# Gates as a diagonal factor in the turning of the dense rows, slot stores one by one, an early second weight group

## The chip, the cores and the metric

The kernel runs on one core of a Trainium2 chip. The metric is device microseconds for one execution, lower is better. The core has a matrix engine (PE, with its weight loads shown as PEld), a vector engine (DVE), an activation engine (ACT), a general engine (POOL), and a queue engine (SP) that issues most transfers. Each engine works through its own instructions in program order, and waits on semaphores of the others.

## The reference

Three stages stand one behind the other, all in float32:

```python
# 1: attention with heads mixed before and after the softmax (4 batches, 12 heads, 448 tokens, 64)
scores = scale * q @ k.T ; scores = einsum('bhij,hg->bgij', scores, w_pre)
attn = softmax(scores)   ; attn = einsum('bhij,hg->bgij', attn, w_post) ; x = attn @ v   # 1792 x 768
# 2: one of 8 experts for each row
logits = normalize(x) @ normalize(expert_emb).T / tau
e = argmax(logits) ; gate = softmax(logits)[e]
x = gate * (relu(x @ w1[e]) @ w2[e])          # w1: 768 x 1024, w2: 1024 x 768
# 3: a dense block
h = x @ w_in ; out = (h - tanh(h)) @ w_out    # w_in: 768 x 2048, w_out: 2048 x 768
```

## The kernel before

**Precision.** Most products run on pairs: a value is split into a rounded high part (ACT copy to fp32r) and a low part (a subtraction on DVE or POOL), and three matmuls (high·high, high·low, low·high) are added up in PSUM. Plain float32 products and turnings by the identity stand beside them.

**Attention** runs in 180 blocks of up to ten query rows of all heads. The scores go through SBUF to a relay transfer on SP, then to the product with w_pre (line 373), the exponential on ACT (line 380), the product with w_post (line 412) and the product with v. At the start, `load_k` brings the keys of four head pairs into four buffers and the last two follow in the loop over pairs; `prep_en` prepares the expert embeddings (its two loads on SP, a square and a root on ACT, a chain of small DVE operations).

**Experts.** Nine items follow: eight experts with room for 256 rows each, and one item for overflow rows ("o"). Rows are fetched by an indirect gather on POOL, turned, multiplied with w1 in eight chunks `h_chunk` (each ends in an ACT relu, line 729), then with w2 in `y_half`. The weights of the next item are loaded by SP (`feed1`, `feed2`) as buffers come free and split on ACT and DVE (`do1`, `do2`). In the chunk loop `pump()` advances a generator by two steps a chunk: it works out the gate and the slot of each row (`emit_G`, `emit_ov`), stores both to DRAM as `sg_d` (twenty small stores on SP, lines 636 and 638, five between two yields), and prepares the overflow item (`ov_src`). Leftover conversion work on w_in and w_out runs in `conv_step`.

**Overflow item.** The results of all experts lie in `y_d` at slots, not yet multiplied by their gates. While the overflow item runs, POOL gathers the rows of the first half of the tokens (seven tiles of 128, `y0_gathers`), in token order. `y0_piece(j, hf)` multiplies tile j in place by its gates (`y_scale`, on DVE for j under 4 and on POOL for the others, line 846), turns three blocks of it by the identity and splits them into the tiles that held w1. These pieces stand between the matmuls of the overflow item (`ov_mid`), with the splits of the first w_in group (`wi0_split`). Then comes a branch, `tc.If(again > 0)`, for a second and further overflow tile and a fuller first half; this input doesn't enter it.

**Dense block.** It has 16 groups (j): two halves of 896 tokens, eight groups of 256 hidden columns. A group has four steps x of `stageA` (18 matmuls each, then ACT: square, tanh, two more squares, then a chain of six DVE operations), and between them 14 calls of `stageB` for the group before (six matmuls each, added up by DVE, line 1391). `between(x, chain)` also carries the splits of the next w_in and w_out group (`work`, line 1322 on ACT and 1323 on POOL), and the pieces of the second half's rows: `y_start` gathers, `y_piece` scales (every second tile on POOL) and turns them, three tiles in group 2, two at the end of group 7 and two at the start of group 8. Dependencies are tracked by tile; the order on each engine is that of the program.

Of the kernel before, what the change touches and what calls it, by code (L numbers as in the profile page):

```python
# [8 lines left out]
F32 = mybir.dt.float32  # L9
# [21 lines left out]
def body(ctx: ExitStack, tc, q, k, v, w_pre, w_post, emb, tau, w1, w2, win, wout, out):  # L31
# [4 lines left out]
    DM = H * D  # L36
# [93 lines left out]
    if True:  # L130
# [5 lines left out]
        LAG = 2  # L136
        NSR = 8
        nat = {}

# [8 lines left out]
        def load_k(b, p):  # L148
            t = ap.tile([CP, NJ, 2, D], F32, tag="natk", name=f"natk{b}_{p}", bufs=4)
            for hh in range(2):  # L150
                sp.dma_start(t[:, :, hh, :], k[b, 2 * p + hh].rearrange("(p c) d -> p c d", c=NJ))
            nat["k", b, p] = t
# [10 lines left out]
        load_q(0, 1)  # L163
        for p in range(1, 4):
            load_k(0, p)
        make_identity(nc, ident)

# [44 lines left out]
        ids0 = cp.tile([128, 1], I32, name="ids0")  # L212
        taub = cp.tile([128, 1], F32, name="taub")
        rtau = cp.tile([128, 1], F32, name="rtau")
# [40 lines left out]
        def prep_en():  # L255
            e0, e1 = xbuf[1][:E], xbuf[0][:E]
            sp.dma_start(e0, emb)
            sp.dma_start(taub, tau.to_broadcast([128, 1]))
            yield
            dve.reciprocal(rtau, taub)  # L260
            yield
            ess = cp.tile([E, 1], F32, name="ess")
            act.activation(e1, e0, AF.Square, accum_out=ess)
            yield
            for rn in inv_norm(ess, E, 1, "e"):
                yield
            dve.tensor_scalar(e1, e0, rn, rtau[:E], ALU.mult, ALU.mult)
# [309 lines left out]
        def emit_ov():  # L577
# [54 lines left out]
            for b in range(B):  # L632
                for it, (i0, n) in enumerate(IT):
                    nb = n // 10
                    r0, t = b * S + i0, 4 * b + it
                    sp.dma_start(sg_d[r0:r0 + 10 * nb, :].rearrange("(m r) k -> r m k", r=nb), sgp[:10 * nb, t, :])
                    if n % 10:
                        sp.dma_start(sg_d[r0 + 10 * nb:r0 + n, :], sgp[10 * nb:n, t, :])
                yield

    with mctx:
        mp, mq = [None], [None]
        keep = {}

        def ld1(src, nm, lo=0, hi=KD):
# [35 lines left out]

        def xsplit(xhl, t, j, hf, nm):
            pt = ps("e" if hf else "d", f"xt{nm}_{j}_{hf}")
            for c in range(3):
                cc = 3 * hf + c
                pe.transpose(pt[:, c * 128:(c + 1) * 128], t[:, cc * 128:(cc + 1) * 128], ident)
# [155 lines left out]

        def y_scale(t, j, eng):
            eng.tensor_scalar(t, t, sgn[:, j, 1:2], None, ALU.mult)  # L846

        def y0_piece(j, hf):
            if hf == 0:
                y_scale(yg0[j], j, dve if j < 4 else pool)  # L850
            xsplit(keep["w1"], yg0[j], j, hf, "y0")

        def wi0_split(x):
            sl = (slice(None), slice(3 * x, 3 * x + 3))
            act.copy(keep["wi0"][0][sl], raw6[sl])
            pool.tensor_sub(keep["wi0"][1][sl], raw6[sl], keep["wi0"][0][sl].bitcast(F32))

        def y0_again():
            yg0.clear()
            y0_gathers()  # L860
            for j in range(HJ):
                for hf in range(2):
                    y0_piece(j, hf)
            for x in range(2):
                wi0_split(x)

# [16 lines left out]

        osrc = []

        def tables():
# [196 lines left out]
        for p in range(NP):  # L1083
            if p + 4 < NP:
                load_k(0, p + 4)
            if p == 1:
# [106 lines left out]
        for n, e in enumerate(items):  # L1193
# [11 lines left out]
            elif e == OV:  # L1205
                y0_gathers()
                d2 = lambda f: lambda: do2(n, f, w2c)
                for f in range(4):
                    do2(n, f, w2c)
                t0 = h_over(hhl, w1c, xhl, 0, nm, {3: [d2(4)]})  # L1210
                t1 = h_over(hhl, w1c, xhl, 1, nm, {1: [d2(5)], 2: [t0], 4: [d2(6)]})
                do2(n, 7, w2c)
                keep["wi0"] = xtile("wi0")
                y0 = [lambda j=j, hf=hf: y0_piece(j, hf) for j in range(HJ) for hf in range(2)]
                ov_mid = [{2: [t1], 3: y0[0:1], 4: y0[1:2], 5: y0[2:3] + [lambda: wi0_split(0)], 6: y0[3:4], 7: y0[4:5]},
                          {f: y0[5 + f:6 + f + f // 7] + ([lambda: wi0_split(1)] if f == 2 else []) for f in range(KF)}]
            else:
                for f in range(KF):
# [4 lines left out]
                    if n == 6:  # L1223
                        pump(100)
                    if n == 7 and f == 2:
                        sp.dma_start(sgn, sg_d.rearrange("(j q) k -> q j k", q=128))
                    if f % 3 == 1:
# [27 lines left out]
        while ncv[0] < NCV or cst:  # L1255
            conv_step()
        again = nc.values_load(ovi[0:1, 2:3], min_val=0, max_val=1)
        with tc.If(again > 0):
            nov = nc.values_load(ovi[0:1, 0:1], min_val=0, max_val=NOV)
            with tc.For_i(1, nov, 1) as ko:  # L1260
                over_alone(ko, "ov")
            y0_again()


    with ExitStack() as dctx:
# [16 lines left out]
        def y_start(j):  # L1282
            yg1[j] = dp.tile([128, DM], F32, tag="yg", name=f"yg{j}", bufs=3)
            y_gather(yg1[j], j)

        def y_piece(j, hf):
# [111 lines left out]
        orr = wo_load(0, act)  # L1398
        wr = wi_load(1, act)
        NG = NF // GF  # L1400
# [6 lines left out]
        for j, (hf, g) in enumerate(seq):  # L1407
# [4 lines left out]
            groups = [(t, nh) for t in range(HT // 128) for nh in range(2)] if prev is not None else []  # L1412
            work = []
            wo_n = wo_tile(g)
            for f in range(GF):
                work.append(lambda f=f, r=orr, w=wo_n: wsplit(w, r, slice(f, f + 1)))
# [55 lines left out]
```

## Time and profile before

| | |
|---|---|
| median of 3 runs | 1386.45 us (1385.5 to 1386.89) |
| the profiled execution | 1384.36 us |
| its span, first to last instruction | 1382.6 us |
| mean granted clock of PE | 0.979 |
| busy: PE, DVE, ACT, POOL | 95%, 72%, 53%, 37% |

The span is what the trace covers; what lies around it is 1.8 us. The profile shows each instruction's start and length on its engine, the line that made it, and for idle time what ended it. "PEclk" and the last columns of a window give the granted clock as a share of 2.4 GHz.

### The profile page before, as it was taken

Reading aid. Unit: us, or ns where it says so; the run is one execution under the profiler, and the core shown is the slowest. Engines: PE = TensorE matmul, PEld = TensorE weight load, DVE = VectorE, ACT = ScalarE, POOL = GpSimd, SP = SyncE. Lnnn points to the kernel's source line nnn. Section 1 sums busy time; section 2 is a strip of 40 time slices with the busy share of each in tenths; the row PEclk is TensorE's granted clock in tenths of the full one; section 3 lists DMA queues with packets and bytes.
Section 4 is the critical chain, followed back from the end, with each engine's and each line's share of the span. In section 5 each row is a group of like instructions: output and inputs, shape, how many; then the busy total and the mean of one; then the engine's idle time right before and its main releaser. Section 6 shows DMA issues by size and latency. Waiting matters only on the chain. (4 is left out here: it accounts for less than half of the span.)

```text
span 1382.6 us, 24798 instructions
## 1 busy us (share of the span) xinstructions
PE 1307.3 (95%) x9036; PEld 1137.6 (82%) x9036; DVE 1001.4 (72%) x2173; ACT 739.1 (53%) x1507; POOL 510.0 (37%) x515
## 2 busy tenths in 40 slices
PE   8999999999999999999799996977999959999998
PEld 5777776776777778999799995777999859999998
DVE  4776787678777767777477773855888737888886
ACT  5666666676666665544344452643444434544442
POOL 0233333333333345332122223633555432454442
PEclk9999999999999999999899999999999979999999
DMA  5886675567556577887787752411212213212102
GB/s 146 253 253 188 186 215 157 173 200 203 157 172 205 161 227 243 265 267 233 218 258 256 243 183 82 126 46 46 61 67 69 65 39 103 69 46 69 46 24 80
DMA packets 153060, 210.93 MB, mean 153 GB/s; under 512 B 57670, under 2 KB 113142, under 8 KB 152934
## 3 DMA queue, kind: packets, MB, share of 16 engines
q1 hardware_dynamic: 148912, 194.22, 45.7%
q0 software_dynamic: 2480, 12.19, 2.6%
q10 hardware_dynamic: 1542, 2.89, 0.6%
q8 instruction: 73, 1.20, 0.4%
q14 instruction: 53, 0.43, 0.1%
HBM read 135.71 MB, written 35.01 MB: 123 GB/s over the span
## 5 line engine op out<-in xcount | busy, mean ns | idle before, releaser
L412 PEld LDWEIGHTS T<-w,p 120*112 120x112 f32 (+1 forms) x1440 | 165.8, 177 | 63.9 <-issue 41.6
L122 POOL TENSOR_TENSOR cm<-cm,ct 128x256 f32<-128x256 f32 x96 | 71.3, 742 | 376.7 <-DVE ct L119 347.1
L412 PE MATMUL T<-w,p 120*112 120x120 f32 (+1 forms) x1440 | 185.1, 272 | 3.1 <-ACT A L417 1.5
L1333 POOL TENSOR_TENSOR gl<-th,gh 128x512 fp32r<-128x512 f32 (+1 forms) x64 | 78.1, 1221 | 268.7 <-ACT gh L1332 207.3
L380 ACT ACTIVATE p<-P,mx 120x448 f32<-120x448 f32 x180 | 114.2, 634 | 117.4 <-DVE mx L387 103.9
L373 PE MATMUL P<-sr,wpre 120*120 120x448 f32 x360 | 166.2, 544 | 1.4 <-ACT p L380 1.4
L1385 PE MATMUL o<-woh,gh 128*128 128x384 f32 x448 | 154.6, 345 | 0.0
L1354 ACT ACTIVATE u<-h 128x512 f32<-128x512 f32 (+1 forms) x64 | 35.0, 546 | 222.6 <-PE h L1352 222.6
L1386 PE MATMUL o<-wol,gh 128*128 128x384 f32 x448 | 152.7, 341 | 0.0
L1387 PE MATMUL o<-woh,gl 128*128 128x384 f32 x448 | 152.5, 340 | 0.0
L1391 DVE TENSOR_TENSOR acc<-acc,o 128x384 f32<-128x384 f32 x196 | 106.3, 547 | 60.3 <-PE o L1387 60.3
L377 DVE TENSOR_REDUCE mx<-P 120x1 f32<-120x448 f32 x180 | 111.4, 619 | 48.7 <-PE P L373 47.0
L417 ACT COPY A<-T 112x480 f32<-112x480 f32 x180 | 101.7, 565 | 15.4 <-PE T L412 14.9
L120 POOL TENSOR_TENSOR cm<-craw 128x256 f32<-128x256 f32 x96 | 64.7, 674 | 92.9 <-DMA craw<-in_moe_w_in 51.6
L726 PE MATMUL hi<-xhi,w1h 128*128 128x256 f32 x336 | 95.4, 284 | 0.0
L727 PE MATMUL hi<-xli,w1h 128*128 128x256 f32 x336 | 95.3, 284 | 0.0
L702 PE MATMUL ypi<-w2hi,hhi 128*128 128x384 f32 x272 | 95.3, 350 | 0.0
L728 PE MATMUL hi<-xhi,w1l 128*128 128x256 f32 x336 | 95.3, 284 | 0.0
L430 PEld LDWEIGHTS AV<-A,v 112*64 112x64 f32 x1536 | 73.9, 137 | 23.9 <-issue 11.4
L703 PE MATMUL ypi<-w2li,hhi 128*128 128x384 f32 x272 | 92.4, 340 | 0.2 <-DVE w2li L673 0.2
L704 PE MATMUL ypi<-w2hi,hli 128*128 128x384 f32 x272 | 92.3, 340 | 0.0
L121 POOL TENSOR_SCALAR cm<-cm 128x256 f32<-128x256 f32 x96 | 85.6, 891 | 8.4
(277 smaller groups left out, 3471.9 us busy)
## 6 DMA issues: line engine op xcount, KB each, us to landing
sr<-ssb SPq DMA_DIRECT2D x176, 210.0 KB
r<-in_moe_w SPq DMA_DIRECT2D x72, 384.0 KB
r<-in_moe_w SPq DMA_DIRECT2D x52, 512.0 KB
craw<-in_moe_w_in SPq DMA_DIRECT2D x48, 256.0 KB
craw<-in_moe_w_out SPq DMA_DIRECT2D x48, 256.0 KB
raw<-wi_d SPq DMA_DIRECT2D x15, 768.0 KB
wor<-wo_d SPq DMA_DIRECT2D x15, 768.0 KB
wi_d<-cm SPq DMA_DIRECT2D x48, 128.0 KB
```

The lines of the kernel that those rows point to most:

```text
L373: pe.matmul(pt[:n, :S], wpre[:n, :n], t[:n, :], start=True, stop=True)
L377: dve.tensor_reduce(mx[:n, 0:1], pt[:n, :S], op=ALU.max, axis=AX.X, negate=True)
L380: return lambda: act.activation(p[:n, :], pt[:n, :S], AF.Exp, bias=mx[:n, 0:1], scale=1.0, accum_out=mx[:n, 1:2])
L412: pe.matmul(pt[:CP, c * n:(c + 1) * n] if m == 10 else pv[:, c], p[:n, c * CP:(c + 1) * CP], w[:n, :] if m == 10 else wv, start=True, stop ...
L417: act.copy(A[T][:, :, :, 10 * r:10 * r + m], tev.pop(i)[1])
L702: pe.matmul(pt[:, :384], a, wh[:, n0:n0 + 384], start=f == 0, stop=False)
L726: pe.matmul(pt[:, :256], wh[:, sl], xh[:, c, :], start=c == 0, stop=False)
L727: pe.matmul(pt[:, :256], wh[:, sl], xl[:, c, :], start=False, stop=False)
L1385: pe.matmul(pt[:, :384], gh[:, sl], wo[0][:, f, n0:n0 + 384], start=f == 0, stop=False)
L1386: pe.matmul(pt[:, :384], gh[:, sl], wo[1][:, f, n0:n0 + 384], start=False, stop=False)
L1387: pe.matmul(pt[:, :384], gl[:, sl], wo[0][:, f, n0:n0 + 384], start=False, stop=f == GF - 1)
L1391: dve.tensor_add(ac[:, n0:n0 + 384], ac[:, n0:n0 + 384], pt[:, :384])
```

## The change

- **Gates.** A gate no longer multiplies the rows: `y_diag` writes the identity times the gates (128 x 128, on DVE), and the turning becomes a float32 product with that diagonal, so it turns and scales at once. For the first half all seven diagonals are made in the overflow item (`y0_diags`); in the dense block one diagonal is made one step ahead of its piece (`y_dg`).
- **Overflow item.** The last four w2 splits, the turnings of the hidden rows and the pieces stand in another order; the last two pieces come behind the overflow item's matmuls (`ov_end`).
- **Second w_in group.** It is loaded on SP ahead of the branch instead of on ACT behind it. A fall into the branch loads and splits the first group anew. In the first dense group the w_in splits come ahead of the w_out splits.
- **Slot stores.** The twenty stores of `sg_d` go into a list, and each chunk of the following items issues one (`sg_store`).
- **Start.** All six key pairs are loaded at once into six buffers; the embeddings and tau are loaded on ACT's queue; ACT does the embeddings' square and root first, and calls one exponential there.

```diff
         def load_k(b, p):
-            t = ap.tile([CP, NJ, 2, D], F32, tag="natk", name=f"natk{b}_{p}", bufs=4)
+            t = ap.tile([CP, NJ, 2, D], F32, tag="natk", name=f"natk{b}_{p}", bufs=NP)
...
-        for p in range(1, 4):
+        for p in range(1, NP):
             load_k(0, p)
+        act.dma_start(xbuf[1][:E], emb)
+        act.dma_start(taub, tau.to_broadcast([128, 1]))
...
         def prep_en():
-            sp.dma_start(e0, emb)
-            sp.dma_start(taub, tau.to_broadcast([128, 1]))
-            yield
-            dve.reciprocal(rtau, taub)
-            yield
             ess = cp.tile([E, 1], F32, name="ess")
             act.activation(e1, e0, AF.Square, accum_out=ess)
-            yield
-            for rn in inv_norm(ess, E, 1, "e"):
+            norm = inv_norm(ess, E, 1, "e")
+            next(norm)
+            act.activation(mxk[:, 0:1], carry[:, 0:1], AF.Exp)
+            yield
+            dve.reciprocal(rtau, taub)
+            yield
+            for rn in norm:
                 yield
...
-                    sp.dma_start(sg_d[r0:r0 + 10 * nb, :].rearrange(...), sgp[:10 * nb, t, :])
+                    sgst.append((sg_d[r0:r0 + 10 * nb, :].rearrange(...), sgp[:10 * nb, t, :]))
...
-                yield
...
-        def xsplit(xhl, t, j, hf, nm):
+        def xsplit(xhl, t, j, hf, nm, dg=None):
...
+                    pe.matmul(pt[:, c * 128:(c + 1) * 128], t[:, cc * 128:(cc + 1) * 128], dg, start=True, stop=True)
...
-        def y_scale(t, j, eng):
-            eng.tensor_scalar(t, t, sgn[:, j, 1:2], None, ALU.mult)
+        def y_diag(t, j):
+            dve.tensor_scalar(t, ident, sgn[:, j, 1:2], None, ALU.mult)
+            return t
...
-            if hf == 0:
-                y_scale(yg0[j], j, dve if j < 4 else pool)
-            xsplit(keep["w1"], yg0[j], j, hf, "y0")
+            xsplit(keep["w1"], yg0[j], j, hf, "y0", dg0[j])
...
+        def sg_store():
+            if sgst:
+                sp.dma_start(*sgst.pop(0))
...
-                t0 = h_over(hhl, w1c, xhl, 0, nm, {3: [d2(4)]})
-                t1 = h_over(hhl, w1c, xhl, 1, nm, {1: [d2(5)], 2: [t0], 4: [d2(6)]})
-                do2(n, 7, w2c)
+                t0 = h_over(hhl, w1c, xhl, 0, nm)
+                t1 = h_over(hhl, w1c, xhl, 1, nm, {2: [t0], 3: [y0_diags, d2(4)], 5: [d2(5)]})
...
-                ov_mid = [{2: [t1], 3: y0[0:1], 4: y0[1:2], 5: y0[2:3] + [lambda: wi0_split(0)], 6: y0[3:4], 7: y0[4:5]},
-                          {f: y0[5 + f:6 + f + f // 7] + ([lambda: wi0_split(1)] if f == 2 else []) for f in range(KF)}]
+                ov_mid = [{0: [d2(6)], 1: [d2(7)], 2: [t1], 4: y0[0:1], 5: y0[1:2] + [lambda: wi0_split(0)], 6: y0[2:3], 7: y0[3:4]},
+                          {f: y0[4 + f:5 + f] + ([lambda: wi0_split(1)] if f == 2 else []) for f in range(KF)}]
+                ov_end = y0[4 + KF:]
...
+        for fn in ov_end:
+            fn()
+        sp.dma_start(raw6, wi_d[:, 256:512].rearrange("(c p) f -> p c f", p=128))
         again = nc.values_load(ovi[0:1, 2:3], min_val=0, max_val=1)
...
-            if not hf:
-                y_scale(yg1[j], j, dve if l % 2 else pool)
...
-                pe.transpose(pt[:, c * 128:(c + 1) * 128], yg1[j][:, cc * 128:(cc + 1) * 128], ident)
+                pe.matmul(pt[:, c * 128:(c + 1) * 128], yg1[j][:, cc * 128:(cc + 1) * 128], dg1[j], start=True, stop=True)
...
-        wr = wi_load(1, act)
+        wr = raw6
...
+            if j:
+                work.extend(wos)
             if nx is not None:
...
+            if not j:
+                work.extend(wos)
...
+                nj = spread.get((j, x + 1) if x < 3 else (j + 1, 0))
+                if nj:
+                    y_dg(nj[0][0])
```

## Rows read from the trace of the kernel before

**Rows 1.** The page, 40 slices of the span, PE's granted clock in tenths.
```profile
PEclk9999999999999999999899999999999979999999
```
**Rows 2.** Waits of PE: waiter, releaser, us in total, times, longest.
```profile
PE yt L1293 <- POOL yg L846: 28.2, 4, 7.8
PE xti L688 <- DVE yi L715: 9.8, 1, 9.8
...
PE yt L1293 <- DVE yg L846: 4.3, 3, 1.9
...
PE h L1352 <- POOL wi1l L1323: 2.8, 2, 1.6
```
**Rows 3.** Timeline of ACT: the first relu of three items in a row.
```profile
633.33 0.38 ACT L729 ACTIVATE hhi<-hi 128x256 fp32r<-128x256 f32 x1 [1.63 <-PE hi L728]
...
681.31 0.38 ACT L729 ACTIVATE hhi<-hi 128x256 fp32r<-128x256 f32 x1 [2.17 <-PE hi L728]
...
716.59 0.38 ACT L729 ACTIVATE hhi<-hi 128x256 fp32r<-128x256 f32 x1 [1.63 <-PE hi L728]
```
**Rows 4.** Timeline of SP: the first slot stores.
```profile
644.48 3.08 SPq L636 DMA_DIRECT2D sg_d<-sgp  x4
```
**Rows 5.** Timeline of ACT: the cast of the next item's last w1 chunk.
```profile
671.01 1.04 ACT L669 CAST w1h<-r 128x1024 fp32r<-128x1024 f32 x1 [11.79 <-DMA r<-in_moe_w]
```
**Rows 6.** Transfers from 640 to 672 us, packets by size.
```profile
DMA packets 4333, 5.93 MB, mean 185 GB/s; under 512 B 2273, under 2 KB 2657, under 8 KB 4331
```
**Rows 7.** Timeline of ACT: the first square of dense groups 2, 3, 4, 7, 8, 9.
```profile
913.52 0.60 ACT L1354 ACTIVATE u<-h 128x512 f32<-128x512 f32 x1 [2.89 <-PE h L1352]
...
964.84 0.60 ACT L1354 ACTIVATE u<-h 128x512 f32<-128x512 f32 x1 [5.86 <-PE h L1352]
...
993.94 0.60 ACT L1354 ACTIVATE u<-h 128x512 f32<-128x512 f32 x1 [5.86 <-PE h L1352]
...
1081.22 0.60 ACT L1354 ACTIVATE u<-h 128x512 f32<-128x512 f32 x1 [5.85 <-PE h L1352]
...
1121.97 0.49 ACT L1354 ACTIVATE u<-h 128x384 f32<-128x384 f32 x1 [4.72 <-PE h L1352]
...
1164.04 0.49 ACT L1354 ACTIVATE u<-h 128x384 f32<-128x384 f32 x1 [4.34 <-PE h L1352]
```
**Rows 8.** Timeline of PE in group 2: the first piece.
```profile
921.43 0.90 PE L1293 MATMUL yt<-ident,yg 128*128 128x128 f32 x3 [6.89 <-POOL yg L846]
```
**Rows 9.** Timeline of POOL in group 2.
```profile
919.17 2.21 POOL L846 TENSOR_SCALAR yg<-yg,sgn 128x768 f32<-128x768 f32 x1
```
**Rows 10.** Timeline of PE in the attention stage: float32 products and turnings.
```profile
152.73 0.86 PE L464 MATMUL X<-ien,xT 128*120 128x136 f32 x6
153.43 0.92 PE L373 MATMUL P<-sr,wpre 120*120 120x448 f32 x2
...
162.87 0.47 PE L303 MATMUL ptq<-ident,natq 120*128 120x120 f32 x3
163.18 0.92 PE L373 MATMUL P<-sr,wpre 120*120 120x448 f32 x2
```
**Rows 11.** Window over the w2 matmuls of expert 7: us, busy (x) by engine, clock, DMA.
```profile
806.00:816.00 10.00, 10.00 (x60) 10.00 (x59) 6.29 (x8) 4.27 (x5) 0.73 (x1) 1.00 0.46 146
```
**Rows 12.** Timeline of DVE in the overflow item.
```profile
828.76 0.68 DVE L756 TENSOR_TENSOR hli<-hqi,hhi 128x512 fp32r<-128x512 f32 x1
829.61 0.96 DVE L673 TENSOR_TENSOR w2li<-r,w2hi 128x768 fp32r<-128x768 f32 x1 [0.16 <-ACT w2hi L669]
```
**Rows 13.** Groups by line: DVE's scaled 120 x 120 tiles of the attention.
```profile
L390 DVE TENSOR_SCALAR w<-wpost,mx 120x120 f32<-120x120 f32 x180 | 67.1, 373 | 6.3
```
**Rows 14.** Timeline of PE: the first dense matmul.
```profile
860.56 0.47 PE L1350 MATMUL h<-w1h,xhwi 128*128 128x512 f32 x1 [1.47 <-DVEq L1258]
```
**Rows 15.** Timeline of ACT at the first block's exponential.
```profile
25.48 1.28 ACT L380 ACT_TABLE_LOAD   x1
```
**Rows 16.** Window over dense group 4, columns as in rows 11.
```profile
993.94:1023.03 29.09, 29.09 (x158) 27.60 (x157) 24.76 (x38) 13.70 (x25) 16.96 (x12) 1.00 0.31 96
```

More of the change, by code (lines that the diff above doesn't have):

```diff
@@ L137, in body @@
         NSR = 8
+        taub = cp.tile([128, 1], F32, name="taub")
         nat = {}
@@ L212, in body @@
         ids0 = cp.tile([128, 1], I32, name="ids0")
-        taub = cp.tile([128, 1], F32, name="taub")
         rtau = cp.tile([128, 1], F32, name="rtau")
@@ L256, in prep_en @@
             e0, e1 = xbuf[1][:E], xbuf[0][:E]
-            sp.dma_start(e0, emb)
-            sp.dma_start(taub, tau.to_broadcast([128, 1]))
+            ess = cp.tile([E, 1], F32, name="ess")
+            act.activation(e1, e0, AF.Square, accum_out=ess)
+            norm = inv_norm(ess, E, 1, "e")
+            next(norm)
+            act.activation(mxk[:, 0:1], carry[:, 0:1], AF.Exp)
             yield
@@ L261, in prep_en @@
             yield
-            ess = cp.tile([E, 1], F32, name="ess")
-            act.activation(e1, e0, AF.Square, accum_out=ess)
-            yield
-            for rn in inv_norm(ess, E, 1, "e"):
+            for rn in norm:
                 yield
@@ L635, in emit_ov @@
                     r0, t = b * S + i0, 4 * b + it
-                    sp.dma_start(sg_d[r0:r0 + 10 * nb, :].rearrange("(m r) k -> r m k", r=nb), sgp[:10 * nb, t, :])
+                    sgst.append((sg_d[r0:r0 + 10 * nb, :].rearrange("(m r) k -> r m k", r=nb), sgp[:10 * nb, t, :]))
                     if n % 10:
-                        sp.dma_start(sg_d[r0 + 10 * nb:r0 + n, :], sgp[10 * nb:n, t, :])
-                yield
+                        sgst.append((sg_d[r0 + 10 * nb:r0 + n, :], sgp[10 * nb:n, t, :]))
     with mctx:
@@ L645, in body @@
         keep = {}
+        sgst = []
         def ld1(src, nm, lo=0, hi=KD):
@@ L687, in xsplit @@
                 cc = 3 * hf + c
-                pe.transpose(pt[:, c * 128:(c + 1) * 128], t[:, cc * 128:(cc + 1) * 128], ident)
+                if dg is None:
+                    pe.transpose(pt[:, c * 128:(c + 1) * 128], t[:, cc * 128:(cc + 1) * 128], ident)
+                else:
+                    pe.matmul(pt[:, c * 128:(c + 1) * 128], t[:, cc * 128:(cc + 1) * 128], dg, start=True, stop=True)
             pv = pt[:, :384].rearrange("p (c t) -> p c t", c=3)
@@ L843, in y_gather, with y0_diags, wi0_split @@
                                     in_offset=bass.IndirectOffsetOnAxis(ap=sgn[:, j, 0:1].bitcast(I32), axis=0))
-        def y_scale(t, j, eng):
-            eng.tensor_scalar(t, t, sgn[:, j, 1:2], None, ALU.mult)
+        def y_diag(t, j):
+            dve.tensor_scalar(t, ident, sgn[:, j, 1:2], None, ALU.mult)
+            return t
+        dg0 = []
+        def y0_diags():
+            t = mp[0].tile([128, DM], F32, tag="xg", name="dg0", bufs=3)
+            u = mp[0].tile([128, OT], F32, tag="osl", name="dg1")
+            for j in range(HJ):
+                dg0.append(y_diag(u if j == 6 else t[:, j * 128:(j + 1) * 128], j))
         def y0_piece(j, hf):
-            if hf == 0:
-                y_scale(yg0[j], j, dve if j < 4 else pool)
-            xsplit(keep["w1"], yg0[j], j, hf, "y0")
-        def wi0_split(x):
+            xsplit(keep["w1"], yg0[j], j, hf, "y0", dg0[j])
+        def wi0_split(x, r=None):
             sl = (slice(None), slice(3 * x, 3 * x + 3))
-            act.copy(keep["wi0"][0][sl], raw6[sl])
-            pool.tensor_sub(keep["wi0"][1][sl], raw6[sl], keep["wi0"][0][sl].bitcast(F32))
+            rv = raw6[sl] if r is None else r
+            act.copy(keep["wi0"][0][sl], rv)
+            pool.tensor_sub(keep["wi0"][1][sl], rv, keep["wi0"][0][sl].bitcast(F32))
         def y0_again():
             yg0.clear()
+            dg0.clear()
+            y0_diags()
             y0_gathers()
@@ L863, in y0_again @@
                     y0_piece(j, hf)
-            for x in range(2):
-                wi0_split(x)
         items = list(range(E)) + ["o"]
@@ L1083, in body @@
         for p in range(NP):
-            if p + 4 < NP:
-                load_k(0, p + 4)
             if p == 1:
@@ L1224, in body @@
                         pump(100)
+                    sg_store()
                     if n == 7 and f == 2:
+                        assert not sgst
                         sp.dma_start(sgn, sg_d.rearrange("(j q) k -> q j k", q=128))
@@ L1261, in body @@
                 over_alone(ko, "ov")
+            raw0 = mp[0].tile([128, FF], F32, tag="r1", name="raw0", bufs=NB1)
+            wiv = wi_d[:, :256].rearrange("(c p) f -> p c f", p=128)
+            for x in range(2):
+                rv = raw0[:, :DM].rearrange("p (c f) -> p c f", c=3)
+                sp.dma_start(rv, wiv[:, 3 * x:3 * x + 3, :])
+                wi0_split(x, rv)
             y0_again()
@@ L1284, in y_start, with y_dg @@
             y_gather(yg1[j], j)
+        dg1 = {}
+        def y_dg(j):
+            dg1[j] = y_diag(dp.tile([128, 128], F32, tag="dg", name=f"dg{j}", bufs=2), j)
         def y_piece(j, hf):
             l = j - HJ
-            if not hf:
-                y_scale(yg1[j], j, dve if l % 2 else pool)
             pt = psb(f"yt{j}_{hf}")
@@ L1412, in body @@
             groups = [(t, nh) for t in range(HT // 128) for nh in range(2)] if prev is not None else []
-            work = []
+            work, wos = [], []
             wo_n = wo_tile(g)
             for f in range(GF):
-                work.append(lambda f=f, r=orr, w=wo_n: wsplit(w, r, slice(f, f + 1)))
+                wos.append(lambda f=f, r=orr, w=wo_n: wsplit(w, r, slice(f, f + 1)))
+            if j:
+                work.extend(wos)
             if nx is not None:
```

## The prediction

> **What bounds the kernel now.** I read the page first. PE is busy for 95% of the span, so a gain can only come from places where PE stands still or runs at its lower clock. The clock line [rows 1] stays at 9 tenths or more except in slice 19 (from 656.7 us; a slice is 34.6 us) and slice 32 (from 1106 us): at the end of the experts' third quarter and at the change of the dense halves. The list of PE's waits [rows 2] says what ended its longest stands: 28.2 us in four waits on rows that POOL scales, 9.8 us in one wait in the expert stage, 4.3 us on rows that DVE scales, 2.8 us on low parts of w_in. The reader is to see that all of these belong to a few places, and that each has a lower clock behind it, so that a wait alone understates its price. I therefore price each place by a period: the distance of one marker to the next, less that of an undisturbed neighbour.
>
> **The slot stores.** From the first relu of one item to that of the next it is 35.28 us undisturbed (681.31 to 716.59) and 47.98 us (633.33 to 681.31) in the item that issues the twenty stores [rows 3]. The difference is 12.70 us. Four stores take SP 3.08 us, 0.77 us each [rows 4]; twenty in a row hold the queue for about 15 us, and the weight loads stand behind them in program order. ACT waited 11.79 us for the last w1 chunk of the next item [rows 5], and PE's 9.8 us [rows 2] end with the copy that frees PE's bank behind it. One store a chunk leaves at most eight in an item, 6.2 us of SP in 35.28 us, each behind one load and not ahead of six. I take the whole 12.7 us as gained; if the stores cost as much wherever they stand, it is 0. Four yields fewer let the overflow item's preparation run two chunks earlier; the pump is idle long before the item needs it, so this costs nothing.
>
> **The dense block's rows.** An undisturbed group takes 29.10 us (964.84 to 993.94) [rows 7]. Group 2, with three tiles, took 51.32 us: 22.2 us more. From the first square of group 7 to that of group 8 it took 40.75 us; group 8 begins with a chain of 384 columns where the others have 512, which is 18 matmuls x 128 columns at 2.4 GHz, 0.96 us, so 28.1 us would be undisturbed, and 12.6 us were lost. Group 8 to 9: 42.07 us, 13.0 us lost. Together 47.8 us [rows 7]. The first piece shows how: PE stood 6.89 us until POOL had scaled its tile [rows 8], and POOL began that 2.21 us operation only at 919.17 [rows 9], since it stands in POOL's queue behind the splits of the same step. The scaling leaves POOL altogether. What takes its place is a 128 x 128 scaling on DVE, nearest to the attention's 120 x 120 tiles at 0.37 us [rows 13], ordered one step (some 7 us) ahead of its piece. DVE is busy 24.76 us of 29.09 in a group [rows 16], so seven of these lie in its free time; without that cover they would cost 2.6 us.
>
> The turnings become dearer. Six records of a float32 product of 136 columns (two records for each product) take PE 0.70 us start to start (152.73 to 153.43); three turnings of 120 columns take 0.31 us [rows 10]. A piece of three products of 128 columns is then 0.70 x 128/136 = 0.66 us, and 14 pieces are 9.2 us that stay on PE. I add 1 us for banks that ACT and DVE free late. The dense rows gain 47.8 - 9.2 - 1 = 37.6 us; bounds are 38.6 us with no wait left, and 25 us if each of the seven tiles keeps 1.8 us (DVE's three waits of today are 1.4 us each [rows 2]).
>
> A rule of the Trainium skill speaks against this edit. On the page "TensorE: Matmul & The Clock Gate", section Terms, the transpose mode is four times as fast for float32 as the ordinary path. By it a piece would take 4 x 0.31 x 128/120, an estimate of 1.3 us, and the 28 pieces would lose some 18 us more than by the row. The attention's products show about twice a turning, not four times; it stays as a rival below.
>
> **The overflow item.** The first dense matmul starts at 860.56 [rows 14]. The new order puts seven diagonals (2.6 us), four w2 low parts (0.96 us each, 3.8 us) and the second low part of the hidden rows (0.68 us) in DVE's queue behind the first one, which ended at 829.44 [rows 12]. If none of it is hidden, PE gets its hidden rows at 836.5; if the diagonals lie in gaps, at 833.9. I take the middle, 835.2, because the relu ahead no longer stands behind a weight cast on ACT. From there PE has the last matmul of one w2 row (0.17 us; 60 matmuls take 10 us [rows 11]), eleven more rows of three matmuls (0.50 us), and thirteen pieces at 0.66 us: 0.17 + 5.5 + 8.6 = 14.3 us, until 849.5. The last piece's copy and low part and the branch follow; the branch alone cost 1.47 us [rows 14], so I take 2.0 us, and the dense block begins at 851.5. Gain 9.1 us, bounds 7.8 and 10.4. The rows were all gathered and are no longer scaled ahead of their turning; POOL keeps only the w_in splits.
>
> **First dense group.** The w_in splits come first and their load is on its way before the branch, so the 2.8 us of waits for w_in low parts [rows 2] go. But the w_out low parts now stand last in POOL's queue, behind the same activations, and the second group's first sums need them. The stall moves from one product to the next. I take 0; bounds are a gain of 4 us and a loss of 2 us. SP's extra load ahead of the branch lies beside the last pieces, and what SP has behind it waits for nothing else.
>
> **Start.** A table load of 1.28 us stands ahead of the first exponential [rows 15]; the early exponential moves it into the start, where ACT has nothing before the first keys have been turned. Part of it lay beside DVE's first maximum. I take 0.6 us, between 0 and 1.3. If the embeddings land late, ACT's early square holds up the first key copies; that costs at most about 1 us, and the six key pairs and two more buffers change nothing that PE waits for.
>
> **The sum.** 12.7 + 37.6 + 9.1 + 0 + 0.6 = 60.0 us. The profiled execution took 1384.36 us, so 1324.4 us; the median of the runs shown is 2.1 us above that execution, so I predict 1326.5 us.
>
> **Rivals.**
> - *A new wait takes the place of POOL's.* In a step with a piece, DVE's queue holds the low part of the piece, which waits for ACT's copy, which stands behind four activations and the weight casts. If PE then waits 1.8 us for each dense tile, 12.6 us are given back: 1339 us. For it: the tiles that DVE scaled had waits too [rows 2]. Against it: those waited for the scaling itself.
> - *The small stores are dear as transfers.* Of the packets around them 2273 of 4333 are under 512 B [rows 6]. If it is these packets and not SP's issuing that held up the weights, spreading gains nothing: 1339 us. Against it: SP issued stores for the whole stretch [rows 4]. The Trainium skill ("DMA: Bandwidth & Descriptors", Specifications) says that under 512 B an engine reads, modifies and writes; this trace has no price for one such packet.
> - *A product costs four times a turning:* 18 us of the gain are lost, 1344 us. Against it: [rows 10]. It decides nothing on the sign.
> - *Slower.* The diagonals stand in DVE's queue behind sums that wait for PE. If each of the 14 tiles made PE wait for its diagonal, the sum turns at 60.0/14 = 4.3 us a tile, and the kernel is measurably slower from 4.5 us. At a whole step of 7.3 us for each it would be 102 us lost and 1428 us. Against it: DVE has 4.3 us free in each group [rows 16], and in the overflow item all seven diagonals come ahead of the first piece.
> - *The gates stay in the way.* If the first pieces waited for the gathers themselves, the scaling would gain nothing but its own time. Against it: POOL's scaling could start at 919.17 only with its rows landed, while the four POOL waits end with POOL.
>
> **How the numbers follow.** The forecast has 0.62, the new wait 0.17, the dear stores 0.12, fourfold products 0.05, waiting for gathers 0.02 (about 1350 us), slower 0.02. The likeliest one's own range comes from its bounds: overflow 7.8 to 10.4, dense up to 38.6, first group -2 to 4, start -0.5 to 1.3, and the 2.1 us between execution and median: 1319 to 1331. To hold eight in ten it reaches to the first two rivals: 1318 to 1340 us. A change of 0.2% (2.8 us) is about what a measurement of this kernel can tell. Faster by more than that 0.97, within it 0.01, slower 0.02.
>
> **What would show it.** The clock line without its 8 and 7. PE's waits without POOL's scaling; the period of the disturbed item at 35.3 us; dense group 2 at about 33 us (29.1 + 6 x 0.66); the first dense matmul some 22 us earlier than now on the trace's own scale (12.7 + 9.1 + 0.6). Wrong would make it: the pieces' products with a wait of their own, a stall in each of three items, or a stall before the second dense group that is longer than today's.

## The result and the profile after

The changed kernel takes 1324.68 us (median of four, 1322.93 to 1325.26), the kernel before in the same comparison 1386.67 us (1385.5 to 1386.99). The ratio is 0.9552, with a 95% interval of 0.9536 to 0.9569: 62 us faster. The profiled execution took 1324.64 us, with a span of 1322.9 us.

The page of the changed kernel: PE's busy time, and the granted clock in 40 slices.
```profile
PE 1299.7 (98%) x9120; PEld 1135.1 (86%) x9120; DVE 1000.5 (76%) x2180; ACT 739.1 (56%) x1508; POOL 495.8 (37%) x508
...
PEclk9999999999999999999999999999999999999999
```
The 8 and the 7 of [rows 1] are gone. PE's waits in the changed kernel: waiter, releaser, us in total, times, longest.
```profile
PE o L1415 <- POOL wol L1352: 3.1, 2, 2.0
...
PE h L1379 <- PEq L1278: 2.5, 1, 2.5
...
PE xti L691 <- DVE yi L720: 0.4, 1, 0.4
```
Against [rows 2], the waits for rows scaled by POOL and DVE (28.2 and 4.3 us) are gone altogether, and the 9.8 us behind DVE's copy of an expert's results are 0.4. The 2.8 us for low parts of w_in are gone too, but 3.1 us for low parts of w_out have come.

ACT's timeline in the changed kernel, the same three relus as in [rows 3].
```profile
630.56 0.38 ACT L734 ACTIVATE hhi<-hi 128x256 fp32r<-128x256 f32 x1 [1.63 <-PE hi L733]
...
665.83 0.38 ACT L734 ACTIVATE hhi<-hi 128x256 fp32r<-128x256 f32 x1 [1.63 <-PE hi L733]
...
701.20 0.38 ACT L734 ACTIVATE hhi<-hi 128x256 fp32r<-128x256 f32 x1 [1.63 <-PE hi L733]
```
The item that took 47.98 us takes 35.27; the next takes 35.37, the one behind it 36.43. PE's timeline at the first dense matmul, then ACT's first squares of dense groups 2, 3, 7, 8 and 9, which answer to [rows 14] and [rows 7].
```profile
836.99 0.47 PE L1379 MATMUL h<-w1h,xhwi 128*128 128x512 f32 x1 [2.50 <-PEq L1278]
```
```profile
892.09 0.60 ACT L1383 ACTIVATE u<-h 128x512 f32<-128x512 f32 x1 [3.42 <-PE h L1381]
...
925.33 0.60 ACT L1383 ACTIVATE u<-h 128x512 f32<-128x512 f32 x1 [5.86 <-PE h L1381]
...
1041.70 0.60 ACT L1383 ACTIVATE u<-h 128x512 f32<-128x512 f32 x1 [5.85 <-PE h L1381]
1072.55 0.49 ACT L1383 ACTIVATE u<-h 128x384 f32<-128x384 f32 x1 [4.74 <-PE h L1381]
1104.40 0.49 ACT L1383 ACTIVATE u<-h 128x384 f32<-128x384 f32 x1 [4.34 <-PE h L1381]
```
Group 2 takes 33.24 us instead of 51.32, groups 7 and 8 take 30.85 and 31.85 instead of 40.75 and 42.07: 38.2 us together. The windows over group 2, before and after (us, then busy and count of PE, PEld, DVE, ACT, POOL, then granted clock, DMA share, GB/s):
```profile
913.52:964.84 51.32, 35.56 (x176) 32.91 (x175) 24.30 (x45) 16.33 (x31) 16.65 (x11) 0.87 0.10 31
```
```profile
892.09:925.33 33.24, 33.24 (x194) 31.75 (x193) 24.76 (x45) 16.06 (x32) 12.75 (x9) 1.00 0.15 48
```
Of the 18.1 us gained here 15.8 are time in which PE stood; the other 2.3 us are busy time, less of it in spite of 18 more matmul records, with the granted clock at 1.00 instead of 0.87. That is why the list of waits understates the price of these places.

These markers split the span into stretches that can be compared between any two kernels here. "Start" is the first relu of the second item; "four items" runs from the first relu of the fourth item to that of the eighth; "overflow" from there to the first dense matmul; "first groups" from there to the first square of group 2; "row groups" is groups 2, 7 and 8 together. Each number is a difference of two such rows in that kernel's trace, in us.

| kernel | median | start | four items | overflow | first groups | row groups |
|---|---|---|---|---|---|---|
| before | 1386.67 | 562.36 | 154.29 | 72.94 | 52.96 | 134.14 |
| changed | 1324.68 | 559.56 | 142.34 | 64.09 | 55.10 | 95.94 |
| changed, once more | 1326.42 | 563.29 | 143.87 | 63.29 | 54.67 | 95.95 |
| stores in one stretch | 1336.28 | 561.89 | **154.09** | 62.73 | 54.66 | 95.94 |
| dense rows scaled at the piece | 1361.14 | 558.47 | 141.64 | 62.98 | 56.23 | **134.27** |
| overflow rows scaled at the piece | 1335.20 | 560.10 | 143.86 | **75.14** | 55.33 | 95.94 |
| start of before | 1327.28 | **561.69** | 143.22 | 63.04 | 54.54 | 95.93 |
| w_in load behind the branch | 1324.48 | 559.18 | 143.48 | 63.93 | **54.73** | 95.94 |
| w_out splits first | 1325.62 | 559.30 | 143.30 | 64.81 | **55.26** | 95.93 |
| all rows scaled ahead on DVE | 1322.65 | 559.04 | 146.47 | **65.42** | 55.14 | **92.10** |
| early splits | 1319.56 | 564.65 | 141.70 | 62.61 | **51.04** | 95.93 |
| stores on ACT | 1322.79 | 558.90 | **142.33** | 62.81 | 55.10 | 95.93 |
| DVE scaling, early splits | 1317.35 | 562.84 | 142.22 | 63.27 | **50.69** | **92.15** |
| the same, stores on ACT | 1315.71 | 558.60 | **141.55** | 62.25 | **50.52** | **92.12** |

Bold is where a kernel was edited. The reader is to see how still the last column stands where nothing was edited (0.02 us), and how far the start and the four items scatter in kernels with the same code there.

### The profile page after: what moved, and what is told of

It is laid out like the page before. It is cut to its first block, busy times and chain, and to the rows that moved or that the text cites. A ratio compares the mean times of both kernels' runs of the same rounds, so it can differ in the third digit from the quotient of the medians.

```text
span 1322.9 us, 24986 instructions
## 1 busy us (share of the span) xinstructions
PE 1299.7 (98%) x9120; PEld 1135.1 (86%) x9120; DVE 1000.5 (76%) x2180; ACT 739.1 (56%) x1508; POOL 495.8 (37%) x508
## 5 line engine op out<-in xcount | busy, mean ns | idle before, releaser
L1414 PE MATMUL o<-woh,gh 128*128 128x384 f32 x448 | 151.8, 339 | 0.0
L1420 DVE TENSOR_TENSOR acc<-acc,o 128x384 f32<-128x384 f32 x196 | 106.4, 547 | 47.6 <-PE o L1416 47.6
L432 PEld LDWEIGHTS AV<-A,v 112*64 112x64 f32 x1536 | 73.9, 137 | 23.9 <-issue 10.7
L1415 PEld LDWEIGHTS o<-wol,gh 128*128 128x128 f32 x448 | 84.7, 189 | 4.9 <-POOL wol L1352 3.8
```

The lines of the kernel that those rows point to most:

```text
L1414: pe.matmul(pt[:, :384], gh[:, sl], wo[0][:, f, n0:n0 + 384], start=f == 0, stop=False)
L1415: pe.matmul(pt[:, :384], gh[:, sl], wo[1][:, f, n0:n0 + 384], start=False, stop=False)
L1420: dve.tensor_add(ac[:, n0:n0 + 384], ac[:, n0:n0 + 384], pt[:, :384])
```

## The experiments

**Stores in one stretch.** SP issues each store where its address is worked out, and the four yields are back.
```
-    sgst.append((sg_d[...], sgp[...]))
+    sp.dma_start(sg_d[...], sgp[...])
...
+    yield
```


> The changed kernel with the twenty slot stores issued in one stretch again, as before. Theory (SP's issuing, 0.77 us a store, holds up the weight loads behind it): the disturbed item has its 48.0 us back instead of 35.3, the two items after it lose their 0.4 us each, so 12 us slower than the changed kernel, about 1336.7 us. Rival (the packets under 512 B are dear wherever they stand): no difference from the changed kernel's 1324.7 us.

Measured: 1336.28 us (1331.75 to 1341.22), ratio to before 0.9634 (0.9603 to 0.9665), which is 11.6 us above the changed kernel by the medians. The disturbed item takes 47.80 us. The cause stands in SP's timeline, here around the loads of the next item's w1 (L930):
```profile
652.65 3.59 SPq L638 DMA_DIRECT2D sg_d<-sgp  x4
656.28 0.47 SPq L640 DMA_DIRECT2D sg_d<-sgp  x1
656.86 0.37 SPq L936 DMA_DIRECT2D r<-in_moe_w  x1
657.28 2.98 SPq L638 DMA_DIRECT2D sg_d<-sgp  x4
...
667.10 2.35 SPq L930 DMA_DIRECT2D r<-in_moe_w  x5
```
and the same loads (L929) in the changed kernel:
```profile
648.21 0.66 SPq L901 DMA_DIRECT2D sg_d<-sgp  x1
...
651.58 8.87 SPq L929 DMA_DIRECT2D r<-in_moe_w  x6
```
In the one the w1 loads begin 34.3 us after the item's first relu (632.77), in the other 21.0 us after it (630.56). The loads are *issued* 13.3 us later, against a loss of 12.5 us in this item. By 663.3 us SP had issued all twenty stores, which took it 14.6 us; the changed kernel has issued four (3.0 us) by the time of these loads. Then the first load stood once more, in SP's waits between 632 and 682 us:
```profile
SPq L930 <- DMA sg_d<-sgp: 3.7, 1, 3.7
```
So some 10 us of the delay are SP's issuing, as the theory has it, and 3.7 us are the landing of a store: the rival, that the small packets are dear as transfers, has that much of it.

**Dense rows scaled at the piece.** `y_dg` is no longer called.
```
+    if not hf:
+        (dve if l % 2 else pool).tensor_scalar(yg1[j], yg1[j], sgn[:, j, 1:2], None, ALU.mult)
-    pe.matmul(pt[...], yg1[j][...], dg1[j], start=True, stop=True)
+    pe.transpose(pt[...], yg1[j][...], ident)
```


> The changed kernel with the dense rows scaled in place at the piece, by POOL and DVE in turn, and turned by the identity, as before; the overflow item keeps its diagonals. Theory (the wait for the scaling in POOL's and DVE's queues is the whole loss): dense group 2 at about 51 us, the dense rows 38 us slower, about 1363 us. Rival (the new order of the first group and the load ahead of the branch carry part of it): less than 30 us slower.

Measured: 1361.14 us (1360.1 to 1361.25), ratio 0.9811 (0.9788 to 0.9834). The three groups take 51.44, 40.77 and 42.06 us, as before to within 0.12 us. PE's waits in group 2 of this kernel:
```profile
PE yt L1324 <- POOL yg L1320: 14.5, 2, 7.6
PE yt L1324 <- DVE yg L1320: 1.3, 1, 1.3
```
So 38.3 us of the three groups hang on this edit alone, as the theory had it; by the medians the kernel is 36.5 us slower than the changed one.

**Overflow rows scaled at the piece.** The same edit in the overflow item, whose new order stays.
```
 def y0_piece(j, hf):
+    if not hf:
+        (dve if j < 4 else pool).tensor_scalar(yg0[j], yg0[j], sgn[:, j, 1:2], None, ALU.mult)
-    xsplit(keep["w1"], yg0[j], j, hf, "y0", dg0[j])
+    xsplit(keep["w1"], yg0[j], j, hf, "y0")
```


> The changed kernel, but the seven tiles of the overflow item scaled in place at their first piece, by DVE (four) and POOL (three), and turned by the identity, as before; the new order of that item and the dense rows' diagonals stay. Theory (the scaling at the piece is the item's loss): from the first relu of the last whole item to the first dense matmul about 72 us again instead of 62.6 to 64.1, 9 us slower, 1334 us. Rival (the new order, with the w2 low parts and the relu's copies placed otherwise, makes most of it): less than 5 us slower, under 1330 us.

Measured: 1335.2 us (1331.89 to 1340.05), ratio 0.9627 (0.9596 to 0.9657). The overflow stretch is 75.14 us, 11 us more than in the changed kernel and 2 more than before. PE's waits in it:
```profile
PE xty L691 <- DVE yg L861: 7.3, 4, 4.4
PE xty L691 <- POOL yg L861: 4.0, 1, 4.0
```
and those of the kernel before:
```profile
PE xty L688 <- DVE yg L846: 7.2, 4, 2.3
PE xty L688 <- POOL yg L846: 4.9, 1, 4.9
```
The changed kernel has neither. The scaling at the piece is the loss, and the new order with that scaling gains nothing. This is the theory; the rival falls. A kernel with the diagonals and the order of before was not run.

**All rows scaled ahead on DVE.** No diagonals, the identity again, but the scaling on DVE and ahead of the piece. In the overflow item two tiles are scaled once the gathers stand in POOL's program, and the others two tiles ahead of their first piece. The edit in the dense block:
```
 def y_dg(j):
-    dg1[j] = y_diag(dp.tile([128, 128], F32, tag="dg", ...), j)
+    dve.tensor_scalar(yg1[j], yg1[j], sgn[:, j, 1:2], None, ALU.mult)
```


> The changed kernel with every row tile scaled in place on DVE one step ahead of its piece and then turned by the identity, no diagonals. Theory A (what helped was to take the scaling off POOL and off the step of its piece; the product with the diagonal is itself a price of PE time, 0.6 us a piece against 0.3 us for a turning): the dense rows gain 14 x 0.3 = 4 us and the overflow item up to as much, 1317 to 1321 us. Theory B (the diagonal is needed, since 0.6 us a tile on DVE and the wait for the gather there delay what is queued behind): same or slower, 1325 to 1332 us.

Measured: 1322.65 us (1319.88 to 1329.14), ratio 0.9538 (0.9512 to 0.9563). The median lies between the two forecasts, and the runs do not separate this kernel from the changed one; the traces say more, and the two places answer differently. In the dense groups theory A holds: 3.84 us less than with the diagonals. A piece in this kernel, and one in the changed kernel, each with the matmul behind it, in PE's timeline:
```profile
905.70 0.49 PE L1325 MATMUL yt<-ident,yg 128*128 128x128 f32 x3
905.94 0.42 PE L1417 MATMUL o<-woh,gh 128*128 128x384 f32 x1
```
```profile
910.26 0.83 PE L1322 MATMUL yt<-dg,yg 128*128 128x128 f32 x6
910.85 0.42 PE L1414 MATMUL o<-woh,gh 128*128 128x384 f32 x1
```
From start to start a turned piece is 0.24 us, a product with the diagonal 0.59 us. In the overflow item the stretch is 65.42 us, where the eleven runs with diagonals there have 62.25 to 64.81. DVE's timeline there:
```profile
819.69 0.64 DVE L857 TENSOR_SCALAR yg<-yg,sgn 128x768 f32<-128x768 f32 x1 [3.73 <-DMA yg<-y_d,sgn]
821.15 0.62 DVE L857 TENSOR_SCALAR yg<-yg,sgn 128x768 f32<-128x768 f32 x1 [0.82 <-DMA yg<-y_d,sgn]
```
The scaling stands in front of DVE's other work until the gathered rows have landed. The seven diagonals need the gates only, and in the changed kernel DVE made them from 812.45 to 814.06, while POOL was still issuing the gathers (809.05 to 819.74). That is theory B's mechanism, and PE's two longest waits in the stretch show what it costs and what it does not:
```profile
PE h L1382 <- PEq L1281: 3.7, 1, 3.7
PE ypi L709 <- DVE hli L761: 2.5, 1, 2.5
```
The second is the wait behind DVE, 0.5 us in the changed kernel. The first is the stand at the branch, 2.0 to 2.5 us in the eleven runs with diagonals. Without the stand at the branch the stretch is 61.7 us here and 60.2 to 62.3 us there, so the cheaper turnings make up for the wait, and one trace does not show that the overflow item needs the diagonals.

**Early splits in the first dense group.** The three w_in splits stand ahead of the first activations, the w_out splits in the first two steps.
```
-    work.append(lambda c=c, r=wr, w=wi_n: wsplit(w, r, slice(c, c + 2)))
+    (work if j else first).append(lambda c=c, r=wr, w=wi_n: wsplit(w, r, slice(c, c + 2)))
+if not j:
+    for fn in first: fn()
...
-    for fn in work[x * len(work) // 3:(x + 1) * len(work) // 3]:
+    for fn in (work[x * len(work) // 3:(x + 1) * len(work) // 3] if j else work[x:x + 1]):
```


> The changed kernel, but in the first dense group the three splits of the second w_in group stand ahead of the first activations and the two w_out splits in the first and second step. Theory (the 3.1 us that PE waits for low parts of w_out at the second group, and DVE's sums that run at half speed beside POOL's splits, are the price of the order): the second group begins on time, first squares of group 0 to group 2 48.2 us apart (19.1 + 29.1) instead of 49.1, and the wait for w_out gone, 1 to 3 us faster: 1321.7 to 1323.7 us. Rival (the second w_in load lands too late, so that ACT stands in front of the first relus): same or up to 2 us slower.

Measured: 1319.56 us (1318.27 to 1324.98), ratio 0.9523 (0.95 to 0.9546). The windows over the first two groups of this kernel (us, then busy and count of PE, PEld, DVE, ACT, POOL, then granted clock, DMA share, GB/s):
```profile
846.14:863.78 17.64, 16.40 (x84) 14.73 (x83) 15.54 (x20) 11.74 (x23) 10.00 (x7) 1.00 0.32 105
863.78:890.94 27.16, 27.16 (x147) 25.68 (x146) 26.64 (x31) 19.13 (x40) 17.45 (x13) 1.00 0.35 113
```
They take 44.8 us instead of 49.1, better than I had expected, and no wait for w_out low parts is left. About half of that is less standing (1.2 us in the two groups against 3.2 in the changed kernel), the rest is busy time at a granted clock of 1.00 where the changed kernel has 0.98 and 0.96. The profiled execution started late (564.65) and took 1323.49 us, so its span shows less of the gain than the median.

**Two parts of the first group undone.** The second w_in group is loaded by ACT behind the branch (`wr = wi_load(1, act)` in place of `wr = raw6`), or the splits stand in the order of before (`work.extend(wos)` first).

> The changed kernel with the second w_in group loaded by ACT behind the branch, as before; the new order of the splits stays. Theory (with w_in split first, its load has to be there early): from the first dense matmul to the first square of the third group 55.1 us now, 56 to 59 us then, 1 to 4 us slower. Rival (the load lands in time behind the branch too, since PE has over 20 us of the first group's products): no difference.

> The changed kernel with the first dense group's splits in the order of before (w_out ahead of w_in); the early load stays. Theory (POOL's queue is the limit, so the order only says which product waits): a wait of 2 to 3 us for low parts of w_in in place of that for w_out, the same time within 1.5 us. Rival (the new order itself costs the 2 us by which the first groups are slower than before): 2 us faster.

Measured: 1324.48 us (1323.76 to 1327.76), ratio 0.9558 (0.9536 to 0.958), and 1325.62 us (1324.8 to 1325.99), ratio 0.9559 (0.9539 to 0.9578). Neither differs from the changed kernel. The first groups take 54.73 and 55.26 us, and PE's waits there are in the kernel with the late load
```profile
PE o L1414 <- POOL wol L1351: 3.1, 2, 2.0
```
and in the kernel with w_out first
```profile
PE h L1381 <- POOL wi1l L1352: 2.7, 2, 1.6
```
The order only says which product waits, and the early load alone is worth nothing measurable.

**Start of before.** Four key buffers, key loads inside the loop, embeddings and tau through SP, no early exponential.
```
-    act.dma_start(xbuf[1][:E], emb)
-    act.dma_start(taub, tau.to_broadcast([128, 1]))
...
-    act.activation(mxk[:, 0:1], carry[:, 0:1], AF.Exp)
```


> The changed kernel with the start of before: four key buffers, later key loads inside the first loop, embeddings and tau loaded by SP, no early exponential. Theory (the edits at the start make the 2.8 us that the ledger shows there): the first relu of the second item comes at about 562.4 instead of 559.6, and the time is 2.8 us longer, 1327.5 us. Rival (the early exponential makes 0.6 us, the rest is how the granted clock fell in the first 17 us of the one profiled execution): 1325.3 us, and the traces of the kernels with either start scatter by 2 us at that marker.

**The changed kernel once more.**

> The changed kernel itself once more, to see how its start and its items with stores scatter. Theory (the granted clock in the first 20 us and late weights in one of three items are not the same in each execution): first relu of the second item within 558.4 and 562, one item of three 0.1 to 5 us long, median 1323 to 1327 us. Rival (both repeat exactly): 559.56 and 36.43 us again.

Measured: 1327.28 us (1326.02 to 1328.07), ratio 0.9569 (0.955 to 0.9588), and 1326.42 us (1322.71 to 1328.6), ratio 0.9558 (0.954 to 0.9576). The first relu of the second item comes at 561.69 with the old start. With the new start it comes at 559.56 and 563.29 in two executions of the very same kernel, and between 558.47 and 564.65 in all twelve traces with that code (median 559.4). The table load did move as meant, from 25.48 to 4.40 us. The first product with w_pre begins between 20.42 and 25.02 us in the twelve traces, so most of the scatter arises ahead of it. The difference of 1 to 3 us between the starts lies within this scatter: it is not settled.

**Stores on ACT.** `act.dma_start(*sgst.pop(0))` in place of `sp.dma_start`.

> The changed kernel with the twenty slot stores spread as they are but issued by ACT, which shares no queue with the weight loads. Theory A (what is left of the stores' price, 0.1 to 4.9 us in one of three items, is SP's issuing time): all items at 35.27 to 35.76 us, 0.8 us faster than the changed kernel, and the runs closer together. Theory B (it is the DMA time of packets under 512 B, which an item with stores takes beside 76% to 82% of its DMA share): the leftovers stay, 0 to 5 us in one item. Rival C (ACT's relus come late behind 0.75 us of issuing): each item with stores 1 to 6 us longer.

Measured: 1322.79 us (1321.34 to 1326.15), ratio 0.9546 (0.9528 to 0.9564). The four items take 142.33 us, 0.8 above the 141.55 of the best; ACT still waits for weights, between 660 and 745 us:
```profile
ACT w1h L671 <- DMA r<-in_moe_w: 3.2, 2, 2.5
```
Rival C falls. Between A and B it is open: with ACT's stores one trace had 0.8 us left and the other (below) none; the ten traces with SP's spread stores have 0.1 to 4.9 us above 141.55.

**The gains together.** DVE scaling of the dense rows ahead (the overflow item keeps its diagonals) with the early splits, and then also the stores on ACT.

> The changed kernel with the dense rows scaled in place on DVE one step ahead and turned by the identity (the overflow item keeps its diagonals), and with the first dense group ordered as in the run with the early splits. Theory: 3.8 us less in the three dense groups with pieces (31.9, 29.45 and 30.75 us for groups 2, 7 and 8) and 1 to 3 us less at the second group: 1318 to 1320 us. Rival (the effects overlap, or the start and the stores scatter more than this): 1321 to 1325 us.

> The dense rows scaled in place on DVE, the early splits in the first dense group, and the slot stores issued by ACT, together. Theory (the gains add, and what the stores still cost is under 1 us): 1316 to 1317.5 us, against 1317.35 us with SP's stores. Rival (ACT's issuing costs as much as SP's): 1317 to 1319 us.

Measured: 1317.35 us (1315.64 to 1319.14), ratio 0.9499 (0.9483 to 0.9515), and 1315.71 us (1312.55 to 1321.93), ratio 0.9505 (0.948 to 0.9529). Both beat the changed kernel by 7 to 9 us: 3.8 in the row groups, about 4.5 in the first groups. Whether the stores on ACT add anything is not told apart.

## Why the prediction was right, point by point

- **Stores, 12.7 us.** Right in the main cause and nearly in size. The disturbed item gave 12.71 us, and 0.76 us came back in the next two items, which I had taken as free: 11.95 us net. Whether those come from SP's issuing or from the transfers is open, since ACT's stores leave as much in one trace. Of the delay with the stores in one stretch, 3.7 us of 13.3 were the landing of a store and not SP's issuing, a part that the working has only as a rival.
- **Dense rows, 37.6 us.** The trace gives 38.2, and undoing this edit alone takes 38.3 back. The feared new wait does not come: no wait on a piece stands among PE's waits, and the seven diagonals took DVE 0.26 to 0.29 us each, less than the 0.37 us of [rows 13]. Of the excess of 47.8 us 9.6 stay, where I had 10.2. What the run with the rows scaled ahead adds is that the diagonal is one way of two: with the scaling off POOL and a step ahead of its piece, plain turnings gain 3.8 us more.
- **A product of 0.66 us a piece.** It is 0.59 us, and 0.24 us for a turning, a ratio of 2.5. The Trainium skill ("TensorE: Matmul & The Clock Gate", section Terms) has four times for float32; by it the 28 pieces would have lost some 18 us more, an estimate, and this trace does not bear it out.
- **Overflow item, 9.1 us.** 8.85 us in the trace, 8.1 to 10.7 in the other ten runs that keep the diagonals (72.94 less each stretch). The run with the scaling back shows that it comes from taking the scaling away from the piece and not from the new order by itself. In the working two small misses cancel: PE has its hidden rows 46.7 us after the item's first relu (772.90 to 819.57) where I had 47.6, and from there to the first dense matmul it takes 17.4 us instead of 16.3, with a stand of 2.50 us at the branch.
- **First dense group, 0 us.** The mechanism was right, but it was not all there is. The stall did move from w_in to w_out (2.8 us before, 3.1 after), which also makes it the longer stall that I had named as a sign of being wrong, by 0.3 us. But the stretch became 2.1 us longer, just past the end of the bounds I gave (a loss of 2). Neither the order nor the early load explains it, since undoing each changed nothing, nor does the later load of w_out on ACT (4.05 us after the first dense matmul, 2.56 before): with the w_in load behind the branch it came 0.59 us after that matmul, and the stretch took 54.73 us. The windows from the first dense matmul to the first square, before and after, show the term that is missing:
```profile
860.56:864.94 4.38, 4.38 (x19) 3.64 (x20) 0.00 (x0) 0.00 (x1) 0.00 (x0) 1.00 0.39 102
```
```profile
836.99:842.99 6.00, 6.00 (x19) 4.81 (x20) 0.00 (x0) 0.00 (x1) 0.00 (x0) 0.72 0.54 155
```
The same 19 records take 1.6 us longer at a granted clock of 0.72: part of the window runs at the lower of its two levels, 1.2 GHz, where these matmuls start 0.43 us apart instead of 0.23. Over the whole stretch PE has 251 records in both kernels and stands 3.2 us instead of 2.9, but is busy 1.8 us longer. When the changed kernel ran once more, the clock was 1.00 in this window and 0.92 in the group behind it, and the stretch took 54.67 us. So the loss is mostly granted clock and hardly the stall; what makes the clock fall in one place or the other is not shown.
- **Start, 0.6 us.** The profiled execution shows 2.8 us, and the runs can't tell it from 0.6.
- **The sum.** 11.95 + 38.20 + 8.85 - 2.14 + 2.80 = 59.66 us on the trace's span, where I had 60.0. The 2.1 us that I had added from the execution to the median came to nothing (1324.64 and 1324.68 us); that is the 1.8 us by which 1326.5 was too long. The close hit owes something to errors of opposite sign: the first groups lost 2.1 us and the start gave 2.2 us more than its term, of which most may be the luck of one execution.

## What to carry to other kernels

A scale by row that comes just ahead of a transposition can go into the matrix of that transposition. What this removes is not work but a wait: the diagonal needs the gates only, so it can be made before the rows are there. It is not the only way. Where there is time to scale ahead on an engine that is free, as here in the dense groups, the plain turning is cheaper for PE (0.24 us against 0.59 us). In the overflow item, where the rows land late, scaling ahead held up DVE's other work, and which of the two is better there one trace doesn't tell.

## What the runs showed of the hardware

**The first 20 us differ from execution to execution.** PE's timeline of two kernels with the same code at the start, the same float32 turnings and the product behind them:
```profile
12.41 0.60 PE L289 MATMUL ptk<-ident,natk 112*128 112x112 f32 x4
12.94 0.47 PE L332 MATMUL S<-kh,qh 64*120 64x448 f32 x2
```
```profile
13.10 1.01 PE L289 MATMUL ptk<-ident,natk 112*128 112x112 f32 x4
14.03 0.73 PE L332 MATMUL S<-kh,qh 64*120 64x448 f32 x2
```
The first is the best kernel, the second the one with early splits, and in the windows of both from 10 to 15 us:
```profile
10.00:15.00 5.00, 5.00 (x39) 3.07 (x37) 3.43 (x12) 4.38 (x8) 0.00 (x0) 1.00 0.61 127
```
```profile
10.00:15.00 5.00, 5.00 (x26) 3.09 (x22) 2.28 (x6) 2.53 (x4) 0.00 (x0) 1.00 0.58 126
```
The granted clock reads 1.00 in both, though PE got through 39 instructions in the one and 26 in the other. The marker at the start scatters by 6.2 us over the twelve traces, so a term of the start of a few us can't be read from one trace.

**Small stores cost DMA time.** Windows over the same item, the fifth, without stores (in the kernel with the stores in one stretch) and with eight (in the changed kernel):
```profile
680.57:715.83 35.26, 35.26 (x254) 35.20 (x253) 27.61 (x53) 17.24 (x28) 10.30 (x11) 1.00 0.78 247
```
```profile
665.83:701.20 35.37, 35.37 (x254) 35.18 (x253) 28.27 (x53) 17.53 (x29) 11.66 (x11) 1.00 0.89 257
```
The DMA share goes from 0.78 to 0.89 for 4% more GB/s. That this is where the late weights come from is not shown.

**An operation of DVE takes longer beside POOL.** DVE's timeline in the changed kernel, the same operation of the same shape:
```profile
848.96 0.76 DVE L1397 COPY_PREDICATED th<-mk,s 128x512 f32<-128x512 uint8 x1
...
854.04 1.71 DVE L1397 COPY_PREDICATED th<-mk,s 128x512 f32<-128x512 uint8 x1
```
and POOL's timeline beside it:
```profile
846.02 1.29 POOL L1352 TENSOR_TENSOR wi1l<-raw,wi1h 128x512 fp32r<-128x512 f32 x1 [16.21 <-ACT wi1h L1351]
850.45 1.58 POOL L1362 TENSOR_TENSOR gl<-th,gh 128x512 fp32r<-128x512 f32 x1 [3.13 <-ACT gh L1361]
851.99 3.16 POOL L1352 TENSOR_TENSOR wi1l<-raw,wi1h 128x512 fp32r<-128x512 f32 x2
```
POOL stands still during the first and splits w_in during most of the second. Over the dense blocks of three kernels (before, changed, early splits) all 55 rows of this operation and shape that POOL leaves alone last 0.74 to 0.82 us, and all 37 that overlap work on POOL last 1.67 to 1.74 us. That the splits make it slower was not tested by a run of its own; it fits the gain of the early splits, which do POOL's work before DVE begins.
